# Attention and mixture of depths on one core: another order for stores, weight blocks, loads, squares, gates and rankings

## The chip, the cores and the metric

The kernel runs on 1 core of one Trainium2 chip. The metric is device time in microseconds (us) of one execution; the times of several executions are given by their median. All data is float32.

## The reference

The kernel computes attention with normalized queries and keys, and then a "mixture of depths": of each batch's 448 tokens, the 128 with the highest gate score go through a two-layer network, and the others pass unchanged.

```python
batch, n_heads, seq, head_dim = (8, 12, 448, 64)        # D = 12 * 64 = 768, F = 1024, capacity = 128

def rmsnorm(x, g):
    rms = np.sqrt(np.mean(x * x, axis=-1, keepdims=True) + 1e-06)
    return x / rms * g
q_n, k_n = (rmsnorm(q, g_q), rmsnorm(k, g_k))
scores = scale * np.matmul(q_n, k_n.transpose(0, 1, 3, 2))
attn = softmax(scores)
x = np.matmul(attn, v)                                  # then (B, S, H*D)

scores = np.einsum('bsd,d->bs', x, w_gate)
out = x.copy()
for b in range(B):
    top_idx = np.argpartition(-scores[b], capacity)[:capacity]
    xe = x[b, top_idx]
    h = np.maximum(xe @ w1, 0.0)
    ye = h @ w2
    g = 1.0 / (1.0 + np.exp(-scores[b, top_idx]))
    out[b, top_idx] = x[b, top_idx] + g[:, None] * ye
```

## The kernel before, in words

**Stages.** The twelve heads of a batch form three groups of four; the eight batches have 24 groups n. The kernel passes through 24 stages q = 0 to 23, and in stage q computes the attention of group n = q in seven units of 64 keys each. A unit is `scores` (four matmuls of 64x448 on PE, L404, then the exponential on ACT, `p`, L413), `values` (L428, p times v into the PSUM tiles `av`) and `add_probs` (L444, DVE adds up the p of the seven units, for the denominator). Of the six additions of a group, the table ARRAY gives the last ones to PE, which then sums several tiles in `sum_keys` (L471, 8 small matmuls for each tile). One stage later the group is finished: `sum_keys`, `invert_sums` (L494, L496), and for each half c of the group's heads `to_tokens` (L526 transposes on PE, L528 writes the tile x on DVE).

**Preparing a group.** Ahead of stage n the queries of group n have to be scaled. `squares` (ACT, L298) squares the tile `tok`; `sum_squares` reduces it on DVE (L330) and POOL raises it to the power -0.5 (L331); this is done for two halves. `rows_out` (L342) sends the norms to a small DRAM buffer, `rows_in` (L354) loads them back, spread over 128 partitions, as `bc`, in two DMAs, and `scale_q` (L363, DVE) multiplies the tile qT in place. The first scores of stage n wait for it. The table PREPARED says when each of these steps is issued.

**After a batch.** When the last group of a batch is in x, `store_x` (L542) writes the batch to the output in one DMA of 1344 KB, `gate` (L554, DVE) multiplies x with the gate's weights, half of the token blocks at a time, `spread` (L567) and `score_rows` (L584) put the scores into rows, `count` (L600) ranks them, `annotate` (L615 to L619) puts rank and gate beside x, and `select` (L627, POOL, indirect DMAs) writes the selected tokens to DRAM, from where `load_selected` (L650) brings them as `xe`. The tables GATES and RANKS say when; batch 1 has its gate from PE (GATE_PE).

**The mixture.** Two batches at a time, `mixture` does both layers with seven products of blocks in place of eight, in 15 steps for a pair of batches. This needs differences of weight blocks: `load_block` (L267) loads the plain blocks, `mix` (L279 to L292) makes the differences once on DVE, `store_mixed` keeps them in DRAM, and `load_mixed` brings them into the `ring`. BLOCKS and MIXED give the times. The products are L753 for the first layer and L823 for the second; L695 adds the result to xe, and POOL writes the rows out (L683). From stage 8 on, one mixture step may follow each of the places 0.6, 0.75 and 0.9 of a stage; the pairs in SKIP have none.

**Order.** No scheduler moves anything: every engine executes its instructions in the order in which the program issues them. Functions are put down with `at(time, function)` and are issued by `run` when the stage reaches that time; 5.4 is place 0.4 of stage 5. Stages below 8 have two places, 0.5 (after units 0 to 3) and 1 (after 4 to 6); later ones have 0.4, 0.6, 0.75 and 0.9. Default times are in `prepare`, `after_tokens`, `ranks_of` and in the loop over n that issues the loads; the tables override them.

**Queues and buffers.** All ordinary transfers are issued by SP, in one order. A DMA that has to wait holds back those behind it. The load of qT n waits for the last scores of stage n - 3, that of v n for the last `values` of stage n - 3; `tok` reuses one of six buffers and waits for the `squares` that read it; `rows_in` waits until `rows_out` has landed. The DMAs of SP share eight semaphores in turn, so that one waits for the eighth before it to land.

Of the kernel before, what the change touches and what calls it, by code (L numbers as in the profile page):

```python
# [17 lines left out]
def _bcast_row(ap_1d: bass.AP, parts: int) -> bass.AP:  # L18
# [1 line left out]

ARRAY = (0, 0, 1, 2, 3, 2, 2, 2, 1, 0, 0, 2, 1, 0, 0, 0, 0, 0, 0, 0, 0, 0, 0, 0)
GATE_PE = {1}
OTHER_BANK = (8, 12, 14, 15, 17, 20, 21)
SKIP = ((8, 0), (8, 1), (8, 2), (11, 2), (13, 2), (14, 1), (16, 2), (18, 2), (19, 2), (20, 1),
 (21, 1), (22, 1), (23, 1), (23, 2))
MIXED = ((1, 1, 0, 8.9), (1, 1, 1, 8.9), (1, 2, 0, 9.9), (1, 2, 1, 10.3), (1, 3, 0, 10.3),
 (1, 3, 1, 10.3), (1, 0, 0, 10.9), (1, 0, 1, 11.6), (2, 1, 0, 11.9), (2, 1, 1, 11.9),
 (2, 2, 0, 12.6), (2, 2, 1, 12.6), (2, 3, 0, 12.75), (2, 3, 1, 14.3), (2, 0, 0, 14.3),  # L30
 (2, 0, 1, 14.6))
BLOCKS = (2.3, 2.73, 3.16, 3.59, 4.02, 4.45, 4.88, 5.31, 4.74, 6.17, 6.6, 8.03, 7.46, 8.14)
LOADS = {('kT', 21): 19.3, ('tok', 15): 10.7, ('v', 18): 16.91}
PREPARED = {3: {'out': 1.3},
 4: {'in': 2.9, 'out': 2.3},
 5: {'in': 3.9, 'out': 3.3, 'sq1': 3.5, 'sum0': 2.92, 'sum1': 3.89},
 6: {'in': 4.9, 'out': 4.3, 'scale': 5.5},
 7: {'in': 5.9, 'out': 5.3},
 8: {'in': 6.9, 'sum1': 6.89},
 9: {'in': 7.9, 'out': 7.3},  # L40
 10: {'in': 8.9, 'out': 8.3},
 11: {'sum1': 9.75},
 13: {'scale': 12.59},
 14: {'scale': 13.4, 'sum0': 11.62},
 15: {'out': 13.75},
 17: {'in': 15.75},
 18: {'in': 16.92, 'out': 16.61},
 20: {'out': 18.89, 'scale': 19.42},
 22: {'out': 20.59},
 23: {'sq0': 20.76}}  # L50
# [12 lines left out]
MAX_SCORE = 60.0
# [54 lines left out]
def fast(  # L118
# [25 lines left out]
    NJ = S // CP  # L144
# [4 lines left out]
    DM = H * D  # L149
# [7 lines left out]
    scale = 1.0 / math.sqrt(D)  # L157
# [236 lines left out]
    probs, sums, avs, xTs, rdens, xs = {}, {}, {}, {}, {}, {}  # L394
# [143 lines left out]

    gates, parts, rowss, highers, ranks, slots_dram = {}, {}, {}, {}, {}, {}

    def store_x(b):
        nc.sync.dma_start(  # L542
            out=out[b].rearrange("(p j) c -> p j c", j=NJ), in_=xs[b][:, :, 0:DM]
        )

    def gate(n, js):
# [325 lines left out]
    def at(slot, fn, *args):  # L872
        todo.setdefault(slot, []).append(lambda: fn(*args))
# [115 lines left out]
    def add_late():  # L989
# [7 lines left out]
        out=gg, in0=loads.gcol[:, 0:1], scalar=scale, in1=loads.gcol[:, 1:2], op0=OP.mult, op1=OP.mult  # L997
# [662 lines left out]
```

## Time and profile before

Four executions took 505.43, 506.60, 500.43 and 504.89 us; the median is 505.16. The profiled execution took 504.17 us, with a span of 502.4.

| engine | busy us | share of the span | instructions |
|---|---|---|---|
| PE, matmul | 480.5 | 96% | 4716 |
| PEld, weight load | 296.6 | 59% | 4716 |
| DVE | 371.5 | 74% | 646 |
| ACT | 285.5 | 57% | 523 |
| POOL | 190.7 | 38% | 104 |

| stage | from, us | to, us |
|---|---|---|
| 2 | 36.56 | 50.35 |
| 4 | 63.37 | 78.31 |
| 5 | 78.31 | 95.36 |
| 6 | 95.36 | 110.78 |
| 7 | 110.78 | 125.30 |
| 8 | 125.30 | 141.17 |
| 9 | 141.17 | 163.72 |
| 10 | 163.72 | 184.64 |

A stage here runs from the first scores of its group to the first scores of the next. The mean granted TensorE clock is 0.986 of full speed. In the profile, a row names the line of the kernel, the engine, the operation, the output and the input, the number of instructions and their time; a bracket gives idle time of the engine just before them and what ended it. "PEclk" is the clock that was granted to TensorE. The trace also tells when each DMA was issued and when it had landed.

### The profile page before, as it was taken

To read this page: it belongs to the slowest core of one execution; us is meant where nothing else is said; L and a number is where in the kernel's file an instruction comes from. 1 tells how busy PE (TensorE), PEld (TensorE's weight loads), DVE (VectorE), ACT (ScalarE), POOL (GpSimd) and SP (SyncE) were. 2 spreads that over 40 slices of the span, in tenths; PEclk is the share of its full clock that TensorE was granted. 3 is DMA by queue.
4 is the path that set the end of the run, shared out by engine and by line. 5 is a ranking of instruction groups with operands and counts; after the bars stand their busy time and mean duration, and the time that the engine had idled before them with its cause. 6 is when DMAs were issued, how large, how long until landed. Compare 5 with 4: busy or idle time off the path is not lost.

```text
span 502.4 us, 11762 instructions
## 1 busy us (share of the span) xinstructions
PE 480.5 (96%) x4716; PEld 296.6 (59%) x4716; DVE 371.5 (74%) x646; ACT 285.5 (57%) x523; POOL 190.7 (38%) x104
## 2 busy tenths in 40 slices
PE   8999999799989999999999999999999999999992
PEld 6553455344538686454456776555655577759951
DVE  5678699564997997888979886889988785742141
ACT  5887877577766757638547576656655653102100
POOL 0785441644663345404644336214445011021003
PEclk9999999899989999999999999999999999999996
DMA  8968999877987795788777797568485504864721
GB/s 299 316 208 274 277 289 325 260 230 247 346 290 243 231 331 172 245 266 307 261 268 250 243 321 253 197 202 301 138 283 191 174 8 141 268 231 158 224 92 67
DMA packets 44865, 118.44 MB, mean 236 GB/s; under 512 B 10147, under 2 KB 10404, under 8 KB 44802
## 3 DMA queue, kind: packets, MB, share of 16 engines
q1 hardware_dynamic: 41170, 110.66, 66.9%
q0 software_dynamic: 3344, 6.71, 3.8%
q8 instruction: 39, 0.64, 0.5%
q10 hardware_dynamic: 288, 0.23, 0.2%
q14 instruction: 24, 0.20, 0.1%
HBM read 93.81 MB, written 31.64 MB: 250 GB/s over the span
## 4 chain that ended last, share of the span: by engine, by line
PE 68%; DVE 3%; issue 1%; DMA 1%; POOL 1%; ACT 0%; POOLq 0%; DVEq 0%; ACTq 0%
PE sc L404 16%; PE av L428 16%; PE moe_ps L753 9%; PE moe_ps L823 8%; PE side_ps L823 6%; PE side_ps L753 6%; PE x_ps L526 3%; PE den_ps L471 2%; PE xeT_ps L729 1%; DMA out_dram<-xe,row 1%; PE row_ps L584 1%; DVE ss L330 1%; POOL out_dram L683 1%; DVE x L528 1%; DVE sum L444 0%
## 5 line engine op out<-in xcount | busy, mean ns | idle before, releaser
L413 ACT ACTIVATE p<-sc,rinv 128x448 f32<-128x448 f32 x336 | 187.8, 641 | 90.7 <-PE sc L404 61.8
L331 POOL TENSOR_TENSOR rinv<-ss,neg_half 128x14 f32<-128x14 f32 x46 | 130.2, 2841 | 156.7 <-DVE ss L330 144.4
L404 PE MATMUL sc<-qT,kT 64*64 64x448 f32 x1344 | 156.4, 549 | 8.2 <-issue 3.4
L428 PE MATMUL av<-p,v 64*64 64x448 f32 x1344 | 151.6, 539 | 0.0
L444 DVE TENSOR_TENSOR sum<-sum,p 128x896 f32<-128x896 f32 x104 | 113.8, 1094 | 5.1 <-ACT p L413 0.7
L428 PEld LDWEIGHTS av<-p,v 64*64 64x64 f32 x1344 | 64.7, 134 | 63.3 <-issue 54.5
L404 PEld LDWEIGHTS sc<-qT,kT 64*64 64x64 f32 x1344 | 59.0, 134 | 71.5 <-issue 42.8
L627 POOL DMA_INDIRECT selected<-x,rank x32 | 40.0, 1249 | 89.6 <-DVE x L619 82.1
L330 DVE TENSOR_REDUCE ss<-sq 128x14 f32<-128x910 f32 x46 | 48.8, 1093 | 3.6 <-ACT sq L298 3.6
L298 ACT ACTIVATE sq<-tok 128x896 f32<-128x896 f32 (+1 forms) x49 | 44.9, 938 | 6.3 <-DVE ss L330 4.2
L528 DVE TENSOR_TENSOR x<-x_ps,rden 112x512 f32<-112x512 f32 x48 | 32.6, 689 | 17.3 <-PE x_ps L526 15.0
L363 DVE SCALAR_TENSOR_TENSOR qT<-qT,gg,bc 128x896 f32<-128x896 f32 x22 | 25.2, 1148 | 14.6 <-DMA bc<-rows 11.8
L554 DVE SCALAR_TENSOR_TENSOR prod<-x,wg 112x448 f32<-112x448 f32 (+1 forms) x56 | 31.2, 556 | 1.4
L526 PE MATMUL x_ps<-ident,xT 128*112 128x128 f32 x192 | 28.5, 275 | 0.4 <-DVE rden L496 0.4
L444 DVE TENSOR_TENSOR sum<-p 128x896 f32<-128x896 f32 x24 | 26.1, 1087 | 3.5 <-ACT p L413 3.4
L683 POOL DMA_INDIRECT out_dram<-xe,row x7 | 8.4, 1202 | 51.9 <-DVE xe L695 45.8
L451 ACT COPY xT<-av 128x448 f32<-128x448 f32 x48 | 23.2, 537 | 4.1 <-PE av L428 3.6
L526 PEld LDWEIGHTS x_ps<-ident,xT 128*112 128x112 f32 x192 | 21.5, 133 | 4.9 <-issue 2.9
L753 PE MATMUL moe_ps<-xeT,ring 128*128 128x128 f32 x192 | 23.2, 277 | 0.2 <-DVE hT L770 0.2
L600 DVE SCALAR_TENSOR_TENSOR cmp<-score_rows,gate,earlier 112x448 f32<-112x448 f32 x32 | 21.8, 683 | 1.7 <-ACT score_rows L590 1.0
L753 PE MATMUL side_ps<-xeT,w 128*128 128x128 f32 x192 | 22.8, 275 | 0.0
L695 DVE SCALAR_TENSOR_TENSOR xe<-moe_ps,xe 128x384 f32<-128x384 f32 x14 | 8.6, 617 | 19.0 <-PE moe_ps L823 18.9
(106 smaller groups left out, 461.2 us busy)
## 6 DMA issues: line engine op xcount, KB each, us to landing
tok<-in_tok_dram SPq DMA_DIRECT2D x47, 448.0 KB, 5.7
ring<-mixed SPq DMA_DIRECT2D x48, 384.0 KB, 4.2
qT<-in_qT_dram SPq DMA_DIRECT2D x24, 448.0 KB, 3.8
kT<-in_kT_dram SPq DMA_DIRECT2D x24, 448.0 KB, 5.9
v<-in_vp_dram SPq DMA_DIRECT2D x24, 448.0 KB, 7.0
out_dram<-x SPq DMA_DIRECT2D x8, 1344.0 KB, 9.4
bc<-rows SPq DMA_DIRECT2D x44, 224.0 KB, 4.3
mixed<-ring SPq DMA_DIRECT2D x16, 384.0 KB, 7.5
```

Source lines behind the costliest of these rows:

```text
L298: nc.scalar.activation(out=sq[:, h, :, 0:D], in_=t[:, h], func=AF.Square, scale=scale)
L330: nc.vector.tensor_reduce(out=ss, in_=sq, axis=AX.X, op=OP.add)
L331: nc.gpsimd.tensor_tensor(out=rinv.rearrange(flat), in0=ss.rearrange(flat), in1=neg_half.to_broadcast([128, 2 * NI]), op=OP.pow,)
L404: nc.tensor.matmul(out=scs[hh][D * c : D * (c + 1), 0:S], lhsT=get("kT", n)[r, c, D * i : D * (i + 1)], rhs=get("qT", n)[r, c, :], start=True,
L413: nc.scalar.activation(out=p[:, hh], in_=scs[hh][:, 0:S], func=AF.Exp, scale=rinvs[n, 1][:, hh, i : i + 1],)
L428: nc.tensor.matmul(out=avs[n][c][D * hh : D * (hh + 1), 0:S], lhsT=get("v", n)[r, hh, i, :], rhs=probs[u][r, hh], start=(i == 0), stop=(i ...
L444: nc.vector.tensor_tensor(out=sums[n], in0=probs.pop(u - 1) if begins else sums[n], in1=probs.pop(u), op=OP.add)
L526: nc.tensor.transpose(out=ps[:CP, j, :], in_=t[:, j, :], identity=ident)
L528: nc.vector.tensor_tensor(out=xs[b][:, :, col : col + 128].rearrange("p j (h d) -> p j h d", d=D), in0=ps[:CP].rearrange("p j (h d) -> p j ...
L627: w = nc.gpsimd.indirect_dma_start(out=t[:, :], out_offset=bass.IndirectOffsetOnAxis(ap=rank[:, j : j + 1], axis=0), in_=x[:, j, :], in_of ...
L753: nc.tensor.matmul(out=ps[:, 128 * f : 128 * f + n], lhsT=w[:, d, 128 * f : 128 * (f + 1)], rhs=h[:, d, :n], start=first and f == d == 0, ...
L823: nc.tensor.matmul(out=ps[:n, c0:c1], lhsT=h[:, f, :n], rhs=w[:, f, c0:c1], start=first and f == 0, stop=(f == HF - 1), skip_group_check=True,
```

## The change

`store_x` gets a slice of the token blocks, and a batch is stored by two DMAs of 672 KB. Batches 0, 3, 5 and 7 issue both at the place of the former store; for batches 1, 2, 4 and 6 the table STORES gives each half a time. All else is a change of tables: which sums PE takes (ARRAY, 16 additions in all as before), which tokens' transposes use another PSUM pool (OTHER_BANK), which places have no mixture step (SKIP, 14 as before), the times of mixed blocks, of plain blocks, of 34 loads, of the steps of preparation, of gates and of rankings. The instructions are the same but for eight more DMAs. In the changed file the functions stand 38 lines further down (`scale_q` is L401 in place of L363).

```diff
-ARRAY = (0, 0, 1, 2, 3, 2, 2, 2, 1, 0, 0, 2, 1, 0, 0, 0, 0, 0, 0, 0, 0, 0, 0, 0)
+ARRAY = (0, 1, 1, 2, 3, 0, 3, 2, 1, 0, 0, 1, 2, 0, 0, 0, 0, 0, 0, 0, 0, 0, 0, 0)
-OTHER_BANK = (8, 12, 14, 15, 17, 20, 21)
-SKIP = ((8, 0), (8, 1), (8, 2), (11, 2), (13, 2), (14, 1), (16, 2), (18, 2), (19, 2), (20, 1),
- (21, 1), (22, 1), (23, 1), (23, 2))
-MIXED = ((1, 1, 0, 8.9), (1, 1, 1, 8.9), (1, 2, 0, 9.9), (1, 2, 1, 10.3), (1, 3, 0, 10.3),
- (1, 3, 1, 10.3), (1, 0, 0, 10.9), (1, 0, 1, 11.6), (2, 1, 0, 11.9), (2, 1, 1, 11.9),
- (2, 2, 0, 12.6), (2, 2, 1, 12.6), (2, 3, 0, 12.75), (2, 3, 1, 14.3), (2, 0, 0, 14.3),
+OTHER_BANK = (8, 14, 20, 21)
+SKIP = ((8, 0), (8, 1), (8, 2), (11, 1), (13, 2), (14, 1), (16, 2), (18, 2), (20, 1), (22, 0),
+ (22, 1), (22, 2), (23, 1), (23, 2))
+MIXED = ((1, 1, 0, 8.9), (1, 1, 1, 9.9), (1, 2, 0, 9.3), (1, 2, 1, 10.3), (1, 3, 0, 10.3),
+ (1, 3, 1, 10.9), (1, 0, 0, 10.9), (1, 0, 1, 11.6), (2, 1, 0, 11.9), (2, 1, 1, 12.6),
+ (2, 2, 0, 12.6), (2, 2, 1, 12.6), (2, 3, 0, 13.6), (2, 3, 1, 14.6), (2, 0, 0, 14.4),
  (2, 0, 1, 14.6))
-BLOCKS = (2.3, 2.73, 3.16, 3.59, 4.02, 4.45, 4.88, 5.31, 4.74, 6.17, 6.6, 8.03, 7.46, 8.14)
-LOADS = {('kT', 21): 19.3, ('tok', 15): 10.7, ('v', 18): 16.91}
-PREPARED = {3: {'out': 1.3},
- 4: {'in': 2.9, 'out': 2.3},
- 5: {'in': 3.9, 'out': 3.3, 'sq1': 3.5, 'sum0': 2.92, 'sum1': 3.89},
- 6: {'in': 4.9, 'out': 4.3, 'scale': 5.5},
- 7: {'in': 5.9, 'out': 5.3},
- 8: {'in': 6.9, 'sum1': 6.89},
- 9: {'in': 7.9, 'out': 7.3},
- 10: {'in': 8.9, 'out': 8.3},
- 11: {'sum1': 9.75},
- 13: {'scale': 12.59},
- 14: {'scale': 13.4, 'sum0': 11.62},
- 15: {'out': 13.75},
- 17: {'in': 15.75},
- 18: {'in': 16.92, 'out': 16.61},
- 20: {'out': 18.89, 'scale': 19.42},
- 22: {'out': 20.59},
- 23: {'sq0': 20.76}}
-GATES = {7: (8.9, 9.4),
- 8: (9.9, 10.4),
- 10: (11.75, 12.6),
- 11: (12.9, 13.3),
- 13: (15.3, 15.4),
+BLOCKS = (3.55, 5.8, 3.16, 3.66, 4.27, 7.95, 7.13, 8.13, 6.24, 10.92, 6.1, 11.03, 9.71, 9.71)
+LOADS = {('kT', 5): 3.3,
+ ('kT', 10): 8.91,
+ ('kT', 11): 9.91,
+ ('kT', 12): 11.0,
...
+ ('qT', 3): 0.3,
+ ('qT', 4): 1.6,
+ ('qT', 6): 3.3,
+ ('qT', 7): 4.6,
+ ('qT', 8): 4.9,
+ ('qT', 9): 6.6,
+ ('qT', 10): 7.21,
+ ('qT', 11): 8.6,
...
+ ('v', 3): 1.91,
+ ('v', 9): 8.0,
+ ('v', 10): 8.61,
...
+PREPARED = {2: {'in': 0.51, 'sum1': 0.91},
+ 3: {'in': 1.5, 'out': 1.3, 'scale': 2.32, 'sq1': 1.3},
+ 4: {'in': 2.9, 'out': 2.3, 'sq0': 1.51},
+ 5: {'in': 3.51, 'out': 3.3, 'scale': 4.32, 'sq1': 3.5, 'sum1': 3.91},
+ 6: {'out': 4.3, 'scale': 5.5, 'sq0': 3.52, 'sq1': 4.29},
+ 7: {'in': 5.51, 'out': 5.3, 'sq0': 4.32},
+ 8: {'in': 6.51, 'out': 6.32, 'scale': 7.5, 'sum1': 6.89},
+ 9: {'sq0': 6.5, 'sq1': 7.5, 'sum1': 7.52},
+ 10: {'scale': 9.89, 'sq0': 7.49, 'sq1': 8.61, 'sum1': 8.61},
+ 11: {'sum0': 8.89},
+ 12: {'in': 10.92, 'scale': 11.74, 'sq0': 9.9},
+ 13: {'in': 11.74, 'scale': 12.6, 'sq0': 10.9, 'sum0': 11.4, 'sum1': 11.61},
+ 14: {'out': 12.62, 'scale': 13.6, 'sum0': 11.74},
+ 15: {'out': 13.62, 'scale': 14.76, 'sq0': 12.89},
+ 16: {'in': 14.74, 'out': 14.59, 'scale': 15.4, 'sq1': 14.4, 'sum1': 14.59},
...
+ 21: {'out': 19.75, 'scale': 20.74},
+ 22: {'out': 20.59, 'scale': 21.75},
...
+STORES = {1: (6.9, 7.5), 2: (9.75, 10.75), 4: (15.75, 16.6), 6: (21.75, 22.6)}
+GATES = {8: (10.4, 10.4),
+ 10: (11.9, 12.75),
+ 11: (12.75, 12.75),
+ 14: (16.3, 16.4),
  17: (18.75, 18.9),
  19: (20.9, 21.3),
- 20: (21.9, 22.4),
- 22: (24.4, 24.4)}
-RANKS = {3: (13.6, 13.6, 13.6, 14.4), 5: (19.6, 20.4, 20.4, 20.9), 6: (22.9, 23.4, 23.4, 23.6)}
+ 20: (21.75, 22.3),
+ 22: (24.3, 24.9)}
+RANKS = {2: (10.9, 10.9, 10.9, 11.3), 5: (19.6, 20.3, 20.3, 20.4), 6: (22.9, 23.4, 23.4, 23.9)}
...
-    def store_x(b):
+    def store_x(b, js):
         nc.sync.dma_start(
-            out=out[b].rearrange("(p j) c -> p j c", j=NJ), in_=xs[b][:, :, 0:DM]
+            out=out[b].rearrange("(p j) c -> p j c", j=NJ)[:, js], in_=xs[b][:, js, 0:DM]
         )
...
         if g == NG - 1:
-            at(s, store_x, b)
+            for js, t in zip((slice(0, 2), slice(2, 4)), STORES.get(b, (s, s))):
+                at(t, store_x, b, js)
```

In BLOCKS, the entries 2k and 2k + 1 are the times of the two parts of block k; blocks 0 to 3 are those of the first layer, 4 to 6 those of the second. In PREPARED, "sq", "sum", "out", "in" and "scale" are `squares`, `sum_squares`, `rows_out`, `rows_in` and `scale_q`.

More of the change, by code (lines that the diff above doesn't have):

```diff
@@ new lines @@
+BLOCKS = (3.55, 5.8, 3.16, 3.66, 4.27, 7.95, 7.13, 8.13, 6.24, 10.92, 6.1, 11.03, 9.71, 9.71)
[3 more added lines that the diff above has]
+ ('kT', 12): 11.0,
+ ('kT', 13): 11.91,
+ ('kT', 14): 12.91,
+ ('kT', 16): 14.7,
+ ('kT', 17): 16.0,
+ ('kT', 18): 16.3,
+ ('qT', 3): 0.3,
[6 more added lines that the diff above has]
+ ('qT', 11): 8.6,
+ ('qT', 18): 15.6,
+ ('qT', 19): 16.6,
+ ('qT', 20): 17.21,
+ ('qT', 21): 18.3,
+ ('tok', 14): 9.5,
+ ('tok', 15): 10.7,
+ ('tok', 19): 15.4,
+ ('tok', 21): 17.4,
+ ('tok', 23): 18.5,
+ ('v', 3): 1.91,
+ ('v', 9): 8.0,
+ ('v', 10): 8.61,
+ ('v', 13): 11.91,
+ ('v', 15): 13.61,
+ ('v', 16): 14.3,
+ ('v', 18): 16.91,
+ ('v', 23): 21.1}
@@ new lines @@
+PREPARED = {2: {'in': 0.51, 'sum1': 0.91},
[13 more added lines that the diff above has]
+ 16: {'in': 14.74, 'out': 14.59, 'scale': 15.4, 'sq1': 14.4, 'sum1': 14.59},
+ 17: {'in': 15.61, 'sum0': 15.39},
+ 18: {'in': 16.92, 'scale': 17.61, 'sq0': 15.4, 'sq1': 16.4, 'sum0': 15.4},
+ 19: {'sq0': 16.91, 'sum1': 17.4},
+ 20: {'out': 18.76, 'scale': 19.42, 'sq0': 17.42},
+ 21: {'out': 19.75, 'scale': 20.74},
+ 22: {'out': 20.59, 'scale': 21.75},
+ 23: {'in': 21.74, 'out': 21.4, 'sum1': 22.6}}
```

## The prediction

> **What bounds the kernel now.** I read the share of busy time first, then the chain that ended last, then the span cut into its 24 stages, and last the waits inside the stages where TensorE lost time.
>
> ```profile
> span 502.4 us, 11762 instructions
> PE 480.5 (96%) x4716; PEld 296.6 (59%) x4716; DVE 371.5 (74%) x646; ACT 285.5 (57%) x523; POOL 190.7 (38%) x104
> PE   8999999799989999999999999999999999999992
> PEclk9999999899989999999999999999999999999996
> PE 68%; DVE 3%; issue 1%; DMA 1%; POOL 1%; ACT 0%; POOLq 0%; DVEq 0%; ACTq 0%
> ```
>
> PE (TensorE) is busy 96% of 502.4 us, so all that an order of the same work can win is in 502.4 - 480.5 = 21.9 us of idle PE, of which the start and the tail (the first digit 8, the last digit 2) hold some 13, and in the few slices where PEclk falls below 9: there the matmuls themselves run longer. The diff changes no matmul count, so I look for idle PE and for lost clock, stage by stage.
>
> The table by stretches has for each stage its length, the busy time of PE, PEld, DVE, ACT and POOL, the granted clock, the DMA share and GB/s. The rows are stages 2, 4, 5, 6, the first 3.4 us of stage 6, stages 7, 8, 9, the first 5.6 us of stage 9, and stage 10:
>
> ```profile
> 36.56:50.35 13.79, 12.71 (x139) 5.47 (x138) 11.36 (x13) 10.58 (x20) 8.59 (x6) 1.00 0.83 270
> 63.37:78.31 14.94, 14.34 (x190) 6.98 (x189) 13.58 (x30) 10.49 (x19) 5.41 (x2) 1.00 0.96 300
> 78.31:95.36 17.05, 14.32 (x202) 7.21 (x202) 10.95 (x24) 11.86 (x22) 9.47 (x6) 1.00 1.01 320
> 95.36:98.80 3.44, 3.44 (x20) 1.40 (x24) 3.30 (x6) 1.27 (x3) 0.91 (x1) 0.51 0.49 119
> 110.78:125.30 14.52, 13.86 (x174) 6.77 (x174) 7.17 (x12) 11.88 (x22) 5.13 (x2) 1.00 0.73 239
> 125.30:141.17 15.87, 13.94 (x173) 8.42 (x174) 15.22 (x27) 10.69 (x20) 10.89 (x6) 1.00 0.89 297
> 141.17:146.80 5.63, 4.99 (x30) 1.75 (x34) 5.49 (x11) 3.16 (x5) 3.63 (x1) 0.70 1.01 384
> 163.72:184.64 20.92, 20.92 (x215) 17.06 (x214) 20.13 (x39) 12.35 (x23) 6.71 (x3) 1.00 0.87 290
> ```
>
> Length less PE busy is what each stage loses: 1.08, 0.60, 2.73 in stages 2, 4, 5; 0.66 and 1.93 in 7 and 8, and nothing in 10. Behind the two long gaps the clock is halved: 3.44 us at 0.51 lose 1.69 us, 5.63 us at 0.70 lose 1.69 us more. The early and middle stages, not the mixture's, hold what can be won.
>
> Who is late there? The timeline of DVE and PE around the ends of stages 5, 7 and 8 (start, length, what; in brackets the idle time before and what ended it):
>
> ```profile
> 94.11 1.15 DVE L363 SCALAR_TENSOR_TENSOR qT<-qT,gg,bc 128x896 f32<-128x896 f32 x1 [5.11 <-DMA bc<-rows]
> 95.36 2.52 PE L404 MATMUL sc<-qT,kT 64*64 64x448 f32 x12 [2.73 <-issue]
> 124.05 1.15 DVE L363 SCALAR_TENSOR_TENSOR qT<-qT,gg,bc 128x896 f32<-128x896 f32 x1 [3.43 <-DMA bc<-rows]
> 139.98 1.14 DVE L363 SCALAR_TENSOR_TENSOR qT<-qT,gg,bc 128x896 f32<-128x896 f32 x1
> 141.17 1.93 PE L404 MATMUL sc<-qT,kT 64*64 64x448 f32 x10 [1.64 <-DVE qT L363]
> ```
>
> Each of these stages starts as soon as `scale_q` (L363) has ended. Before stages 6 and 8, DVE itself idled for `bc`, the norms that `rows_in` loads. SP's issues say why:
>
> ```profile
> 76.28 0.38 SPq L342 DMA_DIRECT2D rows<-rinv  x1
> 78.20 0.69 SPq L542 DMA_DIRECT2D out_dram<-x  x1
> 81.04 2.00 SPq L354 DMA_DIRECT2D bc<-rows  x2
> 109.49 0.33 SPq L110 DMA_DIRECT2D qT<-in_qT_dram  x1
> 112.57 0.38 SPq L342 DMA_DIRECT2D rows<-rinv  x1
> ```
>
> `bc` 6 was issued behind `kT`, `v`, the 1344 KB store of x and two blocks of weights; its second half, issued at 82.0, landed at 94.0, 12 us, where 4.3 is the median of `bc`. `rows` 8 stood behind `qT` 9, which may load only after the last scores of stage 6 (109.49), though the norms of stage 8 were there at 105.6. Before stage 9, `bc` had landed at 137.9, behind the store of batch 1; DVE was then busy with sums until 139.98.
>
> **The change part by part.** ARRAY only moves additions: its sum is 16 before and after. The order of the changed kernel's instructions on SP and DVE, resolved for these stages, gives the rest.
>
> (a) Group 1 gives one of its six additions (1.09 us by L444's row) from DVE to PE. Stage 2 lost 1.08 us waiting for the last sum; it costs 8 more matmuls, 16 took 0.59, so 0.30. Gain 0.8. Groups 5, 6, 11 and 12 change by -2, +1, -1 and +1, so 0.30 comes back, which I leave out; group 5's two additions fall to DVE in stages 5 and 6, where it idled 5.11 us (uncovered, they would cost 2.2).
>
> (b) Two first-layer blocks (2.3 and 2.73) load after stage 3 now and the second layer's mostly 1.5 to 5 stages later; `bc` 5 comes earlier. Stage 4's wait for the gate of batch 0 (0.60) goes if `scale_q` 5 is out of its way: gain 0.6, bounds 0 and 0.7.
>
> (c) `bc` 6 now stands ahead of both halves of the store. `rows` 6 out at about 76.3, SP waits for rows 4.6 us on average (87.3 us in 19), `bc` 4.3: at about 85.2 it is there, 9 us ahead of 94.1. Gain: the gap of 2.73 and the clock's 1.69, 4.4. Behind it `kT` 6 and `v` 6 are ahead in SP's order, the two halves and `qT` 7 and 8 come behind; `qT` 7 is needed 10 us later.
>
> (d) `rows` 8, `kT` 8, `v` 8 and `bc` 8 now stand ahead of `qT` 9. Gain 0.66; DVE gets `scale_q` 8 some 8 us earlier and has less to make up in stage 8.
>
> (e) Because DVE idled 3.43 us and then worked through (15.22 of 15.87 us), `scale_q` 9 came late. With (d) the ranking of batch 1 isn't queued behind `scale_q` 8, the store of batch 1 is cut, and only half of it stands ahead of `bc` 9. The gap of 1.64 goes, stage 9's first wait (5.63 - 4.99 = 0.64) and the clock's 1.69: gain 3.9.
>
> The store in two halves has the same 1344 KB, which took 9.8 us; eight more issues at 0.3 to 0.7 us each lie on SP, which idles longer than that between its waits. Cost 0; without that cover, 8 x 0.69 = 5.5 us over the whole run.
> A page speaks against this: the Trainium skill, "DMA: Bandwidth & Descriptors", section "Bandwidth", asks for transfers of 1 MiB or more for three quarters of the peak rate (measured on another queue than SP's), and its "Anatomy of one DMA" gives about 2.0 us of fixed work to each. Halves of 672 KB break the rule; by the page eight more would add an estimated 16 us if none were hidden. In this trace the 448 KB loads and the 1344 KB store share 320 GB/s in stage 5 with no mark of the small ones being slow, so I add nothing.
>
> New costs. `rows` 7 still waits for POOL (96.27); `bc` 7 was issued from 98.62, 2.3 us later, for 1.2 us, and lands 4.3 later at about 104.1, so `scale_q` 7 ends near 105.5, where stage 7, due at 110.78 and 4.4 + 0.8 + 0.6 earlier now, would begin near 105.0: 0.6, bounds 0 and 2.5. `v` 9 now stands behind `tok` 12, which waits for `squares` 11: landing about 138.5 for a need near 138.3: 0.5, bounds 0 and 1.5. The first half of gate 8 moves into stage 10, counting and annotating to its last place; DVE has 20.13 of 20.92 there already: two products (0.56 each) more make 21.3, and what stands last there delays stage 11's sums: 1.0, bounds 0 and 2.5. `scale_q` 10 and 15 now come behind the second x of stages 9 and 14. In stage 14, x was the last of DVE's work before stage 15 began at 259.60:
>
> ```profile
> 257.02 1.29 DVE L528 TENSOR_TENSOR x<-x_ps,rden 112x512 f32<-112x512 f32 x2
> ```
>
> 257.02 + 1.29 + 1.15 = 259.46 leaves 0.14: 0.3 for the two, bounds 0 and 2. Sum 2.4. Groups 12, 14, 21 and 22 also scale one place later; L363's row gives 1.15 and stage 21's `scale_q` ended 4.6 us early in the trace: 0.
>
> Gains 0.8 + 0.6 + 4.4 + 0.7 + 3.9 = 10.4, costs 2.4, net 8.0. The profiled execution took 504.2 us, so 496.2; the median of the runs shown, 505.2, lies 1.0 above it, so 497.2.
>
> Clock: whether all 3.4 us of lost clock go depends on the gaps that are left. The rows show gaps of 2.73 and 1.64 followed by half clock, and gaps of 0.66 and 1.08 not.
> The Trainium skill, "TensorE: Matmul & The Clock Gate", "Why this matters for your kernels", says that only idle gaps over about 3 us between bursts cost the fast clock. By it, neither gap should have cost it; the trace differs, and the measurement decides. By the page alone, (c) and (e) would bring 3.4 less.
>
> **The rivals.**
> *DVE is the bound from stage 8.* For it: DVE is busy 15.22 of 15.87 and 20.13 of 20.92 in stages 8 and 10. Then `scale_q` 9 stays last, and (e) gives nothing: 10.4 - 3.9 - 2.4 = 4.1, 501.1. Against it: 3.43 us of DVE's idle time in stage 7 is given back.
> *The half clock moves.* A gap over 1.6 us before stage 7, and one in stage 9 for `v` 9, call it back twice: 8.0 - 3.4 = 4.6, 500.6. For it: both transfers are just in time by my working; against it: each gap is worked out under 1 us.
> *Just in time is too late (the slower side).* In the later stages `scale_q` stands later on DVE in six (stages 9, 11, 13, 14, 20 and 21, for groups 10, 12, 14, 15, 21, 22), behind x, and kT, v and bc come later too. If it ends after the last mixture matmul there, each costs what stage 9 cost: 1.64 + 0.64 + 1.69 = 4.0. From two such stages it eats the gain; with four: 16 - 8.0 = +8.0, 513.2. For it: only 0.14 is left before stage 15. Against it: before, `scale_q` ended 4 to 11 us early in these stages, and a move of one place is 2 to 4 us.
> *The loads don't move.* If SP's waits for lanes, not the order, hold `bc` 6, (c) is gone: 501.6. Against it: the order puts it 1344 KB ahead, 4.3 us at 320 GB/s.
>
> **How the numbers follow.** The forecast has 0.55, DVE as bound 0.13, the half clock 0.12, loads that don't move 0.08, too late 0.12. The forecast's own range is 491 to 503: gains at their upper bounds and no costs give 505.2 - 10.5 = 494.7, the idle PE that I haven't named (21.9 - 13 - 7.0 = 1.9) and as much off the tail bring 491; costs at their bounds (8.5) give 503.3. The range of 491 to 506 takes in the middle rivals and leaves out most of the slower case. The runs shown spread from 500.4 to 506.6, so 1% (5.05 us) is about what a measurement of this kernel can tell from no change. Faster by over 1% is below 500.1: 0.53 of the forecast's 0.55 and somewhat under half of the three middle rivals' 0.33, together 0.68; slower (over 510.2) 0.10; the rest 0.22.
>
> **What would show it.** Right: stage 6 starts with no PE gap over 0.7 and a clock of 1.00; `bc` 6 lands before 88 us; DVE doesn't idle for `bc` 8; stage 9 follows stage 8 without 1.64. New waits, if any: PE for `scale_q` 7, for `v` in stage 9, for `scale_q` before stages 10 and 15. Wrong: a half clock in any later stage, or idle PE over 1 us in stages 10 to 22, where the changed kernel would give back what it won.

## The result, and the profile after

The changed kernel takes 501.76 us in the median of 52 executions (498.15 to 505.55), where before takes 504.79 in 78. The ratio is 0.9946, 95% interval 0.9934 to 0.9959: 2.7 us less, a third of the 8.0 that were forecast. (Ratios here leave out a few executions in a slower state of the chip and so differ a little from the quotients of the medians.) The direction held, the size didn't. The profiled execution took 500.23 us.

From the page of the changed kernel: the span, the engines, and the granted clock in 40 slices.

```profile
span 498.4 us, 11755 instructions
PE 479.3 (96%) x4716; PEld 294.5 (59%) x4716; DVE 371.2 (74%) x646; ACT 284.7 (57%) x523; POOL 190.8 (38%) x104
PEclk9999999999989999999999999999999999999997
```

One of the two dips in the clock is gone. The table by stretches (length, busy time of PE, PEld, DVE, ACT and POOL, clock, DMA share, GB/s) has stages 2, 4, 5, 6, 8, the first 5.65 us of stage 9, and stage 12:

```profile
36.02:49.04 13.02, 13.02 (x154) 5.85 (x153) 10.14 (x13) 10.56 (x20) 7.66 (x6) 1.00 0.77 270
62.06:76.23 14.17, 14.17 (x190) 7.02 (x189) 11.62 (x28) 11.21 (x20) 5.12 (x2) 1.00 0.89 292
76.23:90.40 14.17, 14.17 (x202) 7.10 (x201) 13.08 (x26) 10.42 (x21) 6.61 (x5) 1.00 0.71 233
90.40:105.81 15.41, 13.90 (x155) 6.24 (x154) 8.82 (x11) 11.15 (x20) 9.82 (x4) 1.00 0.84 274
120.49:134.95 14.46, 13.63 (x174) 6.78 (x174) 12.31 (x16) 10.60 (x19) 10.88 (x6) 1.00 0.76 242
134.95:140.60 5.65, 5.01 (x29) 1.63 (x33) 5.51 (x11) 3.16 (x5) 3.65 (x2) 0.71 0.91 298
197.03:218.88 21.85, 20.73 (x178) 10.30 (x178) 18.79 (x30) 11.13 (x20) 7.89 (x3) 1.00 0.93 319
```

Set beside before, stages 2 and 4 have no idle PE left, and stage 5 takes 14.17 in place of 17.05. Stage 6 is as long as it was, 15.41 to 15.42: the half clock has gone, and a gap before stage 7 stands in its place. Stage 8 is 1.4 shorter. Stage 9 still opens with the clock at 0.71. Stage 12, 20.90 before, is 1.0 longer. The timeline around these places (the functions are 38 lines further down than before):

```profile
104.55 1.15 DVE L401 SCALAR_TENSOR_TENSOR qT<-qT,gg,bc 128x896 f32<-128x896 f32 x1 [3.89 <-DMA bc<-rows]
105.81 1.74 PE L442 MATMUL sc<-qT,kT 64*64 64x448 f32 x16 [1.51 <-issue]
133.15 0.69 DVE L566 TENSOR_TENSOR x<-x_ps,rden 112x512 f32<-112x512 f32 x1 [1.71 <-PE x_ps L564]
133.75 1.14 DVE L401 SCALAR_TENSOR_TENSOR qT<-qT,gg,bc 128x896 f32<-128x896 f32 x1
134.95 1.93 PE L442 MATMUL sc<-qT,kT 64*64 64x448 f32 x10 [0.83 <-DVE qT L401]
215.72 0.65 PE L564 MATMUL x_ps<-ident,xT 128*112 128x128 f32 x4 [1.12 <-DVE rden L534]
```

The span is 4.0 shorter than that of before; 0.5 of it lies ahead of the first scores, which begin at 9.5 to 10.3 in the profiles of these kernels and their variants, and isn't the change's. So this pair of profiles has 3.5 where 8.0 were forecast. That is not the whole story: other executions of this program look quite different in stage 5, as the experiments found.

### The profile page after: what moved, and what is told of

Its sections match the earlier page's. It is cut to its first block, busy times and chain, and to the rows that moved or that the text cites. A ratio compares the mean times of both kernels' runs of the same rounds, so it can differ in the third digit from the quotient of the medians.

```text
span 498.4 us, 11755 instructions
## 1 busy us (share of the span) xinstructions
PE 479.3 (96%) x4716; PEld 294.5 (59%) x4716; DVE 371.2 (74%) x646; ACT 284.7 (57%) x523; POOL 190.8 (38%) x104
## 4 chain that ended last, share of the span: by engine, by line
PE 91%; DVE 4%; issue 2%; ACT 1%; DMA 1%; POOL 1%; POOLq 0%; DVEq 0%; ACTq 0%
PE sc L442 27%; PE av L466 25%; PE moe_ps L791 9%; PE moe_ps L861 7%; PE side_ps L791 6%; PE side_ps L861 6%; PE x_ps L564 4%; PE den_ps L509 4%; PE xeT_ps L767 1%; PE warm_ps L129 1%; PE row_ps L622 1%; DMA out_dram<-xe,row 1%; PE den_ps L532 1%; POOL out_dram L721 1%; ACT p L451 1%
## 5 line engine op out<-in xcount | busy, mean ns | idle before, releaser
L369 POOL TENSOR_TENSOR rinv<-ss,neg_half 128x14 f32<-128x14 f32 x46 | 128.8, 2814 | 155.2 <-DVE ss L368 129.2
L665 POOL DMA_INDIRECT selected<-x,rank x32 | 41.7, 1302 | 82.4 <-DVE x L657 75.1
L401 DVE SCALAR_TENSOR_TENSOR qT<-qT,gg,bc 128x896 f32<-128x896 f32 x22 | 25.2, 1146 | 6.5 <-DMA bc<-rows 6.5
L791 PEld LDWEIGHTS moe_ps<-xeT,ring 128*128 128x128 f32 x192 | 22.1, 192 | 0.5 <-issue 0.5
```

Of the source, the lines that this page charges most:

```text
L369: nc.gpsimd.tensor_tensor(out=rinv.rearrange(flat), in0=ss.rearrange(flat), in1=neg_half.to_broadcast([128, 2 * NI]), op=OP.pow,)
L665: w = nc.gpsimd.indirect_dma_start(out=t[:, :], out_offset=bass.IndirectOffsetOnAxis(ap=rank[:, j : j + 1], axis=0), in_=x[:, j, :], in_of ...
L791: nc.tensor.matmul(out=ps[:, 128 * f : 128 * f + n], lhsT=w[:, d, 128 * f : 128 * (f + 1)], rhs=h[:, d, :n], start=first and f == d == 0, ...
```

## The experiments

The kernels ran on five chips, numbered here in the order of time, and the kernel before ran on each of them. So ratios to before are compared, and medians only on the same chip. Tables of different length move the line numbers of edited kernels by up to some 70 lines; the operands name the instructions.

| chip | kernel | median us | ratio to before, 95% interval |
|---|---|---|---|
| 1 (before 506.51) | before, `bc` 6 ahead of the store | 506.19 | 1.0007 (0.9970 to 1.0044) |
| 1 | changed, late tables of before | 504.61 | 0.9958 (0.9927 to 0.9989) |
| 1 | changed, other PSUM pool in stage 8 | 504.65 | 0.9972 (0.9949 to 0.9994) |
| 1 | changed, first half of group 7's norms ahead of the selection | 502.54 | 0.9919 (0.9891 to 0.9947) |
| 2 (before 506.25) | changed | 505.36 | 1.0019 (0.9988 to 1.0050) |
| 2 | changed, store of batch 0 later | 504.53 | 0.9967 (0.9929 to 1.0004) |
| 2 | the same with the norms ahead | 502.53 | 0.9933 (0.9895 to 0.9972) |
| 3 (before 504.93) | changed | 501.70 | 0.9950 (0.9917 to 0.9984) |
| 3 | changed, selection of batch 0 later | 496.92 | 0.9857 (0.9813 to 0.9900) |
| 3 | changed, four earlier indirect DMAs | 501.43 | 0.9920 (0.9880 to 0.9959) |
| 3 | changed, no sums of group 4 on PE | 503.41 | 0.9981 (0.9952 to 1.0011) |
| 4 (before 506.16) | changed | 504.73 | 0.9992 (0.9960 to 1.0025) |
| 4 | changed, selection later | 499.67 | 0.9896 (0.9846 to 0.9945) |
| 4 | before, selection later | 507.19 | 1.0043 (1.0007 to 1.0079) |
| 4 | before, selection later and `bc` 6 ahead of the store | 502.37 | 0.9935 (0.9899 to 0.9971) |
| 5 (before 504.68) | changed, four earlier indirect DMAs | 499.80 | 0.9913 (0.9880 to 0.9945) |
| 5 | changed, selection later and two small edits | 498.95 | 0.9879 (0.9839 to 0.9919) |

**Part (c) alone.** The kernel before, with `rows_in` of group 6 at its default place, ahead of the store of batch 0:

```diff
- 6: {'in': 4.9, 'out': 4.3, 'scale': 5.5},
+ 6: {'out': 4.3, 'scale': 5.5},
```

> The kernel before with one edit: bc 6 issued at 4.5, ahead of the store of batch 0, in place of 4.9. Theory, the prediction's part (c) holds for the gap, 2.7, and for the clock of stage 6, 1.7, but 1.5 to 2 come back as a gap before stage 7, since bc 7 waits for POOL as before: 504.8 - 2.7 = 502.1. Rival 1, nothing comes back: 500.4. Rival 2, SP's order isn't what held bc 6 (it is held by the lanes or by the DMA engines' load): 504.8, and bc 6 lands after 90.

It measured 1.0007: nothing, where the theory had 2.7 us. Yet the edit did its work: `bc` 6 was issued at 80.7, the store after it, and DVE never waited for `bc` 6. Stage 5 was as long as ever for another reason:

```profile
77.95:96.66 18.71, 15.97 (x203) 7.62 (x202) 13.11 (x26) 11.11 (x22) 10.00 (x6) 1.00 0.92 294
96.66:110.44 13.78, 13.78 (x186) 6.61 (x185) 7.84 (x10) 10.49 (x20) 5.12 (x2) 1.00 0.84 252
```

Stages 5 and 6 are the rows; with 13.78, stage 6 has lost its gap and its half clock, as (c) wanted, and stage 5 has taken 18.71 with 2.74 of idle PE: short pauses with "issue" in the bracket, that is, nothing that the profile shows. This is called the stall below.

**The late tables, the other pool, the norms.** Three edits of the changed kernel, meant for the losses that its first profile shows. The first has the former tables for everything issued from stage 9 on (SKIP, GATES, RANKS, MIXED, OTHER_BANK, and the late entries of the others). The other two:

```diff
-OTHER_BANK = (8, 14, 20, 21)
+OTHER_BANK = (14, 20, 21)
...
- 7: {'in': 5.51, 'out': 5.3, 'sq0': 4.32},
+ 7: {'in': 5.51, 'out': 5.3, 'sq0': 4.32, 'sum0': 4.89},
```

> The changed kernel's tables for all that is issued before stage 9 (and its blocks), the former tables from stage 9 on. Theory 1, the late tables give back what the front wins: stages 11 to 14 of the changed kernel lost 2.0 us against before (0.1, 0.95, 0.4, 0.5), so this kernel takes about 2 us less than the changed one: 499.8, 0.990 of before; its stage 12 has no wait of PE for rden. Rival, the late tables are neutral and the missing time is lost in stages 6 to 9: 501.8 within 0.6, as the changed kernel.

> The changed kernel with the transposed tokens of group 7's second half in the other PSUM pool (stage 8 taken out of OTHER_BANK), so that the first scores of stage 9 needn't wait 0.64 us until DVE has read them. Theory, the half clock in stage 9 follows from the two idle pieces of 0.83 and 0.64 us around ten scores: without the second the clock stays at 1.00, gain 0.64 + 1.69 = 2.3: 499.5. Rival, the half clock belongs to the sparse end of stage 8 and comes anyway: the clock over the first 5.6 us of stage 9 stays near 0.7, gain at most 0.6: 501.2. Third: the other pool is still in use by the sums of stage 8 and PE waits there: no gain or a loss of up to 1.

> The changed kernel with the sum of squares of group 7's first half issued ahead of the selection of batch 0 (4.89 in place of 4.93), so that POOL raises it to the power before its 6 us of indirect DMAs. Theory, the gap of 1.51 us before stage 7 stands only on bc 7, whose norms waited for POOL until 95.1: they are there some 7 us earlier, bc 7 lands before 100, stage 7 follows stage 6 without a gap: 500.3. Rival, the selection of batch 0 comes 2.8 us later, and its rows hold up SP or the ranking: half or none of the gain, 501.0 to 502.

The late tables: 504.61, on a chip where the changed kernel itself didn't run, so the 2 us can't be read from the median. The profiles have it. Stages 11 to 22 of before, of the changed kernel and of this one, and stage 10 of this one:

```profile
184.64:404.89 220.25, 220.02 (x2109) 128.91 (x2108) 186.20 (x309) 136.32 (x252) 87.61 (x41) 1.00 0.71 237
178.67:401.00 222.33, 220.80 (x2110) 132.10 (x2109) 187.50 (x319) 135.96 (x252) 91.26 (x42) 1.00 0.73 242
185.11:405.37 220.26, 220.03 (x2109) 129.29 (x2109) 186.27 (x309) 136.44 (x252) 86.71 (x41) 1.00 0.72 241
162.86:185.11 22.25, 21.72 (x214) 16.40 (x213) 21.60 (x44) 12.44 (x23) 7.26 (x5) 1.00 0.81 277
```

The late tables cost 2.1 us from stage 11 on, as theory 1 said, and the wait for rden, the group's inverted sums, in stage 12 is gone with them. But stage 10, where the new tables meet the former ones, took 22.25 in place of 20.92, so only 0.7 of it is won. The other pool: stage 9 ran in 20.04 us without idle PE and at full clock, but PE waited in stage 8 for the pool (15.88 in place of 14.46): the third outcome, no gain. The norms: 502.54, and not by the expected way. SP stood on `qT` 8, which waits for the last scores of stage 5, until 93.05, so `rows` 7 left at 94.0, hardly earlier than the 95.2 of the first profile, and DVE still waited 2.0 us for `bc` 7. What the edit moved was POOL's selection of batch 0, 1.0 us later against the sums of group 4, and that seems to have mattered: stage 5 of the other two kernels took 18.64 and 21.24 us, of this one 17.11, where the first profile has 14.17.

**The same two kernels again, and the store.** The store's halves were put at 5.9 and 6.5; one more kernel has the store and the norms.

```diff
-STORES = {1: (6.9, 7.5), 2: (9.75, 10.75), 4: (15.75, 16.6), 6: (21.75, 22.6)}
+STORES = {0: (5.9, 6.5), 1: (6.9, 7.5), 2: (9.75, 10.75), 4: (15.75, 16.6), 6: (21.75, 22.6)}
```

> The changed kernel itself, beside the other kernels of this call, with a profile. In the runs so far on this chip four kernels with bc 6 ahead of the store lost 3 to 7 us in stage 5, where TensorE or ACT stood still with nothing to wait for; the changed kernel's own profile shows nothing of it. Theory 1, the stalls belong to bringing bc 6 and the store together and show here too: 0.4 us in stage 5 of that profile was a lucky execution; expected some 504, and a profile with 3 us or more lost in stage 5. Rival, the edits of those kernels brought the stalls: this one shows less than 1 us, about 503.5 beside 506.5 of before.

> The kernel before itself, once more with a profile on this chip. Theory: its stage 5 loses 3.3 us as in the first profile, to bc 6 or to a stall of instructions, one hiding the other; so what taking bc 6 ahead of the store wins is on average less than 2.7 us. Rival: it shows the first profile's waits to 0.5 us.

> The changed kernel with the two halves of batch 0's store issued at 5.9 and 6.5 in place of 4.5. Theory, while the store runs (80 to 90 us) the instruction blocks of TensorE and ACT come late, and the engine that runs dry stops: without the store in stage 5 the stalls there go, stage 5 takes 14.2 us, the median is 2 to 4 below that of the changed kernel in the same call. Rival 1, the many small matmuls of the sums of group 4 use up the instructions whatever the DMAs do: the stalls stay, no difference. Rival 2, the stall follows the store into stage 6: no difference either, but stage 6 is longer.

> Both edits together, the sum of squares of group 7 ahead of the selection and the store of batch 0 at 5.9 and 6.5. If the two losses are separate they add: 1.5 below the kernel with the store alone, some 500 where the changed kernel takes 504. Rival: the store now stands in front of bc 7 or delays it, and the gap before stage 7 comes back: no better than the store alone.

On this chip, the second, the changed kernel was no faster than before. Its stage 5 took 21.45 us, and that of before, too, had the stall: 20.30 us (17.05 in its first profile), and DVE had no wait for `bc` 6, which was there before the stall had ended. So the stall hides the wait for `bc` 6. It came as theory 1 for the changed kernel expected, but not for its reason: `bc` 6 and the store together are not the cause, as the kernel before, where `bc` 6 comes late, has the stall too. The store alone isn't the cause either: without it in stage 5, the stall was there unchanged (21.12). The kernel with both edits was 2.0 below that with the store alone, as the kernel with the norms had been 2.1 below the other two on chip 1; its gap before stage 7 stayed, 1.26.

What the stall looks like, in the changed kernel's profile on chip 4: POOL's selection (the first, third and last of its four indirect DMAs), and the sums of group 4 on TensorE, each row a group of matmuls (the trace has two records for each).

```profile
84.79 1.16 POOL L665 DMA_INDIRECT selected<-x,rank  x1 [10.15 <-DVE x L657]
...
87.52 0.95 POOL L665 DMA_INDIRECT selected<-x,rank  x1 [0.30 <-issue]
88.77 0.94 POOL L665 DMA_INDIRECT selected<-x,rank  x1 [0.31 <-issue]
...
86.83 0.37 PE L509 MATMUL den_ps<-p,pick_pair 128*32 128x112 f32 x3 [0.33 <-issue]
87.56 0.41 PE L509 MATMUL den_ps<-p,pick_pair 128*32 128x112 f32 x5 [0.36 <-issue]
88.27 0.40 PE L518 MATMUL den_ps<-xT,hT 128*32 128x112 f32 x5 [0.31 <-issue]
89.00 0.41 PE L518 MATMUL den_ps<-xT,hT 128*32 128x112 f32 x5 [0.33 <-issue]
```

Every 0.73 us PE executes some 5 records of small matmuls in 0.4 us and stands for 0.3, waiting for nothing that the profile shows ("issue"). In the first profile, 48 such records took 1.33 us. In seven profiles the pauses began about 1 us after the first indirect DMA of batch 0's selection had begun and ended 0.7 to 0.9 us after the fourth had ended; ACT and DVE stood idle meanwhile, waiting for PE by the profile. In the two kernels with the norms ahead, where the selection met scores, ACT and DVE stood still for 3.7 to 5.6 us, though the tiles from PE that they read next had been there for most of it.

The pauses are not all of the cost. In five of these nine profiles the granted clock fell to a half around their end, for 3.41 or 6.83 us. That is 1.7 or 3.4 us of what the stall cost; the rest, over the 14.2 that stage 5 takes without it, is 2.9 to 4.5.

**Selection or matmuls.** Four kernels on one chip: the changed one, one with the selection moved, one with a dummy selection in stage 2, and one with fewer small matmuls.

```diff
-RANKS = {2: (10.9, 10.9, 10.9, 11.3), 5: (19.6, 20.3, 20.3, 20.4), 6: (22.9, 23.4, 23.4, 23.9)}
+RANKS = {0: (4.9, 4.9, 5.9, 6.5), 2: (10.9, 10.9, 10.9, 11.3), 5: (19.6, 20.3, 20.3, 20.4),
+ 6: (22.9, 23.4, 23.4, 23.9)}
...
+    def warm_select():
+        t = dram_pool.tile([CAP, DM], F32, name="warm_selected", bufs=1)
...
+                out_offset=bass.IndirectOffsetOnAxis(ap=token_i[:, j : j + 1], axis=0),
+                in_=wg[:, :],
...
+    at(2.6, warm_select)
...
-ARRAY = (0, 1, 1, 2, 3, 0, 3, 2, 1, 0, 0, 1, 2, 0, 0, 0, 0, 0, 0, 0, 0, 0, 0, 0)
+ARRAY = (0, 1, 1, 2, 0, 0, 3, 2, 1, 0, 0, 1, 2, 0, 0, 0, 0, 0, 0, 0, 0, 0, 0, 0)
```

The move takes five short DVE instructions and the load of the selected tokens with it.

> The changed kernel again, as the measure for the other three kernels of this call. If the stall in stage 5 is the rule, its profile loses 4 us or more there and the median is 505; if the first profile was the rule, it loses 0.4 us there and the median is 500 to 502.

> The changed kernel with the annotation and selection of batch 0 at 5.9 in place of 4.9 (and its tokens loaded at 6.5). In six profiles with a stall, it began about 1.1 us after POOL's first indirect DMA (82.9 to 86.1) and ended about 1 us after the fourth. Theory 1, the first selection starves the other engines of instructions: the stall moves with it, to the end of stage 5 or into stage 6, and stage 5's sums run in 2 us; the time is the same, or 2 us less where the stall meets scores (as in the kernel with the sum of squares moved). Theory 2, the many small matmuls of group 4's sums use up TensorE's instructions: the stall stays at 84 to 89. Beside it, the powers of group 7 come ahead of the selection on POOL and the gap before stage 7 (0.3 to 1.5) goes under both.

> The changed kernel with four more indirect DMAs on POOL in stage 2, into a buffer that nothing reads (row numbers from the token table, the gate's weights as data), so that the selection of batch 0 is no longer the first use. Theory 1a, it is the first use that starves the engines: the stall moves to stage 2 and is smaller or as large there, and stage 5 takes 14.2. Theory 1b, it is this selection with its surroundings: stage 5 stalls as before, and stage 2 doesn't. Later selections in the same profiles came without stalls, which speaks for 1a.

> The changed kernel with no additions of group 4 on TensorE (ARRAY 3 to 0 there): 24 small matmuls fewer in stage 5's sums, three additions of 1.09 us more on DVE in stages 4 and 5. Theory 2, the burst of small matmuls is the cause: no stall in stage 5, 3 to 5 us less, less 0.5 to 1 for DVE. Theory 1: the sums end at about 84.5 before the selection has begun to bite, and the stall meets the transposes, scores and values after them as it did where the selection came later: 2 to 3 us lost in place of 4.5 to 5, and ACT and DVE stand still too.

Here the changed kernel's profile had no stall, and of its twelve executions nine took 499.1 to 502.3 at a mean clock of 0.989 to 0.994, three 504.8 to 506.4 at 0.985 to 0.987. If those three are the ones that stall, which no profile shows, the median of a kernel depends on how many of its executions do. The moved selection took 496.92, 0.9857 of before: 4.8 us less than the changed kernel, where theory 1 had 2 at most and 1.5 for the gap before stage 7. Most of that can't be the stall, if the changed kernel mostly had none here. Stage 6 of the changed kernel and of the moved selection:

```profile
91.22:107.31 16.09, 13.91 (x155) 6.26 (x154) 8.83 (x11) 11.16 (x20) 9.82 (x4) 1.00 0.83 270
90.42:103.91 13.49, 13.08 (x154) 5.84 (x153) 10.61 (x17) 11.27 (x20) 9.20 (x6) 1.00 0.95 314
```

The gap of 2.18 before stage 7 is gone, since now the powers of group 7 come ahead of the selection on POOL; stage 12 gave another 1.3 in this pair. Stage 5 took 14.17 in both. The kernel with fewer matmuls told nothing of theory 2: the additions given to DVE stood behind the ranking there, and PE waited 5.28 us for the last sum, a plain new wait of my own making.

**Does the stall follow the selection?** On the fourth chip, with the kernel before too:

> The changed kernel, as the measure for this call: 500 to 502 where the stall of stage 5 is rare, 504 to 506 where it is the rule.

> The changed kernel with the selection of batch 0 at 5.9, again beside the changed kernel. Theory, the selection in stage 5 is what holds the gain: 497 on any chip, 0.985 of before, stage 5 at 14.2 us and stage 6 at 13.5, no stall. Rival, the stall belongs to the chip and comes elsewhere: 500 or more, with a loss of 3 us or more in some stage from 5 to 8.

> The kernel before with only the selection of batch 0 moved (4.9 to 5.9; its tokens loaded at 6.5). Theory: the stall of stage 5 goes, but bc 6 is still behind the store and ends stage 5 (2.7 us and the half clock), so 1 to 3 us are won: about 503 where before has 505. Rival, the selection alone made the 8 us: 498.

> The kernel before with both, the selection moved and bc 6 ahead of the store. Theory: now (c) shows: 3 to 4.5 us less than with the selection alone, some 499 to 500, where the edit for bc 6 without the selection's move gave 0. Rival: bc 6 ahead of the store is worth nothing here either, as the kernel with the selection alone.

Here the changed kernel's profile has the stall, and its median is 3.0 us above that on chip 3. Stages 5 and 6 of it, of the changed kernel with the selection later, of before with the selection later, and of that with `bc` 6 ahead of the store:

```profile
78.18:98.03 19.85, 17.72 (x202) 8.03 (x202) 13.07 (x26) 10.41 (x21) 10.46 (x6) 0.91 0.55 175
98.03:111.56 13.53, 13.09 (x154) 5.89 (x154) 8.82 (x11) 11.29 (x20) 5.49 (x2) 1.00 0.96 313
```

```profile
77.72:91.89 14.17, 14.17 (x203) 7.11 (x202) 12.43 (x21) 10.43 (x21) 6.33 (x2) 1.00 0.62 210
91.89:106.79 14.90, 13.64 (x154) 5.97 (x153) 10.05 (x16) 11.38 (x20) 10.10 (x6) 1.00 0.91 294
```

```profile
78.94:96.11 17.17, 14.32 (x202) 7.21 (x202) 10.30 (x19) 11.85 (x22) 6.44 (x2) 0.99 1.00 322
96.11:113.60 17.49, 16.46 (x186) 7.52 (x186) 11.61 (x19) 9.92 (x19) 10.41 (x6) 0.92 0.53 161
```

```profile
79.11:93.35 14.24, 14.24 (x202) 7.18 (x201) 12.46 (x21) 11.11 (x22) 6.45 (x2) 1.00 0.95 329
93.35:109.25 15.90, 14.46 (x187) 6.91 (x186) 9.45 (x16) 10.71 (x20) 9.20 (x6) 1.00 0.77 217
```

The stall follows the selection. In all three kernels with the selection later, stage 5 has none, and the same broken rows of PE stand in stage 6, just behind the selection (94.6 to 99.6, pauses from 98.1 to 100.5 in the second). There they cost less: stage 6 takes 14.90 where the profile without stall had 13.49. The sums of stage 6 are 32 records of small matmuls in the second kernel's trace, where those of stage 5 are 80; whether that is why wasn't tried by itself.

The two kernels from before settle part (c). With the selection later alone, before loses both: stage 5 waits for `bc` 6 again (17.17, as in its first profile), and the stall comes on top in stage 6 (17.49). It is 0.4% slower than before, where 1 to 3 us less were expected. Adding the edit for `bc` 6 wins 1.0043 to 0.9935, 507.19 to 502.37, 4.8 us, where with the selection in its former place (on chip 1) it won nothing. The prediction had 4.4, and stages 5 and 6 of the two profiles, 34.66 and 30.14, have 4.5.

**First use, and a last version.** The dummy selection again, and the moved selection with the two small edits (8 out of OTHER_BANK, the mixed block (2, 1, 1) at 11.9 in place of 12.6):

> The changed kernel with four more indirect DMAs on POOL in stage 2 into a buffer that nothing reads, again. If the first use stalls the engines: no stall in stage 5 in any execution, stage 5 takes 14.2 us, about 501 to 502 with 1 us lost in stage 2 or 3, whichever the chip. If it is this selection: stage 5 loses 5 to 7 us and the median is 505 or more on a chip where before takes 506.

> The changed kernel with the selection of batch 0 at 5.9, group 7's second half transposed in the other PSUM pool (stage 8 out of OTHER_BANK) and the mixed block (2, 1, 1) at 11.9 as before. Each by itself: 5 us, 1.2 (stage 9 at 20.0 in place of 21.2 to 22.8), 0.4 to 1.4 (PE's wait for rden in stage 12). If they add: 0.983 to 0.986 of before, about 498 where before takes 506. Rival: what stages 9 and 12 win comes back in stages 13 to 17 as 0.8 us of new waits, and it is as fast as the moved selection alone, 0.987 to 0.99.

With a dummy selection ahead, stage 5 took 14.17 us in both profiles on two chips. Of the second, stages 2 and 3 in which the dummy runs, and stage 5:

```profile
36.15:49.17 13.02, 13.02 (x155) 5.85 (x154) 9.81 (x11) 10.57 (x20) 11.11 (x10) 1.00 0.77 261
49.17:62.19 13.02, 13.02 (x155) 5.85 (x154) 8.13 (x9) 10.60 (x20) 7.48 (x4) 1.00 0.93 300
76.36:90.53 14.17, 14.17 (x203) 7.10 (x202) 13.06 (x26) 10.44 (x21) 6.65 (x5) 1.00 0.80 254
```

Of twelve other profiles with the selection in stage 5 (without that of the fewer matmuls), nine show the stall. That speaks for the first use of POOL's indirect DMA as the cause; the later selections of every profile come without such pauses, too. But the expectation that the stall would move to the dummy failed: stages 2 and 3, where the dummy is the first use, lost nothing to it in either profile. And two profiles prove little: the changed kernel has no stall in its profile on one of these chips and didn't run on the other. So the cause stays open. One more sign is in the profiles. In all nine with the stall the third indirect DMA takes POOL 0.94 to 0.95 us, as in the rows above; in the three without it, and behind the dummy, it takes 2.1 to 2.3, as here in the first profile:

```profile
85.58 2.08 POOL L665 DMA_INDIRECT selected<-x,rank  x1 [0.30 <-issue]
```

So the stall goes with four indirect DMAs at full pace; which of the two makes the other isn't shown, and the selection moved to stage 6 ran at that pace without pauses on chips 3 and 5.

The two small edits gave nothing: 0.9879, between the two results of the moved selection alone, and its profile shows why. With the block mixed at 11.9, DVE waits 4.0 us for its two loads, everything behind it on DVE is late, and PE waits 2.58 for rden in place of 1.1; stage 12 took 25.0.

The fastest version here is the changed kernel with the selection of batch 0 at 5.9: 0.9857 and 0.9896 of before on two chips, against 0.9950 and 0.9992 of the changed kernel on the same chips.

## Why the prediction was right or wrong

The direction was right, and 2.7 of 8.0 came. Two steps failed. In the pair of first profiles, neither of which has the stall, 3.5 of 8.0 came, and most of what is missing is (e). In executions with the stall, (c) is missing as well.

- **(a), (b):** 0.8 and 0.6 forecast; stages 2 and 4 of the profile are each 0.77 shorter and have no idle PE. Right, though for (a) with luck: 0.30 for the tile given to PE came from a halved row, as if 16 records were 16 matmuls. The trace has two records for each, so 16 are the 8 of one tile. In stage 2 PE's busy time rose by 0.31 all the same (12.71 to 13.02); in stage 5 three tiles took 1.33, 0.44 each.
- **(c), 4.4: the step that failed where the stall comes.** The order on SP did what was said, and the wait for `bc` 6 went. What failed was "Gain: the gap of 2.73 and the clock's 1.69": it counts the wait as if nothing else could take the time of stage 5. The stall, which no term had, makes stage 5 3 to 7 us longer whether or not `bc` 6 is there, so (c) was worth nothing on chip 1, and 4.8 us on chip 4 with the selection out of the way. Where the stall doesn't come, stage 5 won 2.9 and stage 6 the 1.7 of clock. The row that I took for the cost of `bc` 6 holds only where stage 5 has no stall; on chip 2 the kernel before had the stall and no such wait. The spread of the four times, 500.4 to 506.6, was a sign that executions differ by a term that one profile can't show; I used it for the resolution of the measurement only.
- **`bc` 7:** 0.6 forecast, 1.51 measured, 0.3 to 2.2 in other profiles, in the bounds. It landed at about 104.5 (104.1 forecast); stage 6 was ready for it earlier than I had worked out, as ARRAY takes two tiles, some 0.8 us of PE's sums, out of stage 6, and I had left its shifts out of account.
- **(d), 0.7:** stage 8 follows stage 7 without a gap, as forecast, but nothing was won by it: stage 7 takes 14.68 in place of 14.53. One tile of sums more, 0.4, and 0.5 more in scores and values fill it; the second I didn't follow up.
- **(e), 3.9: the step that failed in every profile.** Stage 8 won 1.4, stage 9 lost 0.25 in the pair, 1.2 in all. What failed was "the gap of 1.64 goes". I had taken DVE's lateness for its cause, and (d) did make DVE early: the row at 133.15 has it idle for 1.71 us just ahead. But `scale_q` 9 stands behind an x in DVE's order, and this x waits for PE's transposes; so the gap went to 0.83 only, in all thirteen profiles with these tables and this PSUM pool. Whether `scale_q` 9 ahead of that x would close it wasn't tried. The wait of 0.64 for x in stage 9 has nothing to do with (d) and stayed. The clock, 1.69, was credited to the gaps. It stayed at 0.71 in this profile and was 1.00 in three others of the same program with the same two gaps, as the row below from chip 2 shows.

```profile
140.94:146.60 5.66, 5.02 (x45) 2.04 (x48) 5.52 (x11) 3.60 (x7) 3.67 (x2) 1.00 0.91 319
```

- **Late costs, 1.3 for stages 10 to 15 and 0.5 for `v` 9:** the places named cost nothing; stage 10 took 20.92 as before, `scale_q` 10 and 15 were in time, and PE didn't wait for `v` 9. The cost came in stage 12, where DVE's rden comes late (1.12 of idle PE in the row shown), in stage 13, 0.4, where PE has one tile of sums more, and in stage 14, 0.5, which I didn't follow up. From the start of stage 10 to that of stage 23 it was 2.1 in the pair of profiles.
- **The rivals:** none had the stall. "The half clock moves" did not come: behind the gap of 1.51 before stage 7 the clock stayed at 1.00, and the half clock of stage 9 is that of before. "DVE is the bound from stage 8" was right that `scale_q` 9 stays last, but not for its reason: DVE idled just before. "Just in time is too late" and "the loads don't move" did not come.
- **The store in halves:** cost 0 forecast, and no wait of PE for the halves shows in the profile. A kernel with the changed order and the whole store wasn't tried, so it isn't shown whether whole or halved is better.

## What to carry to other kernels

A wait that one profile shows at the end of a stage may stand beside another one that is as long, and taking away the first brings only what is left over; before such a wait is counted as a gain, ask what else ran in that stretch, and look at a second profile on another chip. When executions of a program spread by more than the gain that is hoped for, look for the term behind the spread: here one number, the place of one selection, was worth 5 us, on chip 4 through the stall, on chip 3 in good part through the gap before stage 7, and a schedule of some hundred numbers 2.7. That an engine was late when a step came late doesn't make it the cause; ask what stands ahead of the step in the engine's order. An experiment that undoes one edit tells little where two costs cover each other; all four combinations of the two edits told it, though not all on one chip.

## What the hardware showed that I had not expected

While POOL issued the first selection's indirect DMAs (four in 5 us), TensorE worked in bursts of about 5 matmul records each 0.73 us in seven of twelve profiles, and in two more ACT and DVE stood still beside scores; later selections did no such thing. That instructions come late is an inference from "issue" as the only releaser; the profile names none. The packets of the instruction queue don't settle it: in stage 5 one of 16 KB took 0.96 us with the stall on chip 4, and 0.97 without it in the first profile. How often it comes differs between chips: perhaps three of twelve executions of the changed kernel on chip 3, going by time and clock, and a median 3 to 4 us higher on chips 2 and 4, where before is 1.2 to 1.3 higher, too.

The half clock is no fixed price of a gap. The same program with gaps of 0.83 and 0.64 us before and in stage 9 ran on at 0.71 in one execution and at 1.00 in three others, and the kernel before with `bc` 6 ahead of the store at 1.00 behind gaps of 2.29 and 0.64. Between the start and the tail the clock records of all twenty profiles show it in stretches of 3.41 us, or twice that, and in no other length; one such stretch at half speed costs 1.7 us of matmuls.
